# All matmuls of the middle units as 64x64 tiles, and the last projection piece in token halves

## The chip, the core and the metric

The kernel runs on one core of a Trainium2 chip. The metric is the device time of one launch in microseconds (us), as the median of several runs; lower is better. The core has a matrix engine (TensorE, PE in the profile, whose weight loads have a row of their own, PEld), a vector engine (VectorE, DVE), a scalar engine (ScalarE, ACT), a general engine (GpSimd, POOL) and a queue engine (SyncE, SP) that here only starts transfers. Each takes its instructions in the order in which the program gives them and waits at each for semaphores. TensorE writes to PSUM, from where only VectorE and ScalarE read; everything else lies in SBUF or in device memory.

## The reference

The input is 8 sequences of 4,096 tokens of 192 values. A causal convolution over 7 tokens runs along each sequence, with softmax weights that the 24 channels of a head share; then every token goes through a gated feed-forward layer:

```python
out = np.einsum('hk,bskhg->bshg', softmax(weight), windows_of_7(x))   # 8 heads, 7 taps
x = out.reshape(32768, 192)
gate = np.maximum(x @ w_gate, 0.0)        # 192 -> 1536
val = x @ w_val                           # 192 -> 1536
result = (gate * val) @ w_out             # 1536 -> 192
```

The kernel computes in fp16 with fp32 sums.

## The kernel before, in words

The sequences are taken in pairs, one of the lower four and one of the upper four, called streams: their channels lie one above the other in the 128 partitions, 64 of the one and 64 of the other, in three chunks of 64 channels. The work is cut into 16 units of 1,024 tokens of both streams, numbered 0 to 15, each of two windows of 512 tokens. Units 0 and 15 take paths of their own (`project`); units 1 to 14 are the middle units and all alike.

A unit's gate and value products (`gate_val`, once per window) go over 12 blocks of 128 hidden features. For each block there are two PSUM tiles of two banks, one for the gate and one for the value, a bank for each stream. For each chunk and stream one matmul (L547) multiplies 64 channels by 128 features over 512 tokens. The two streams' matmuls lie in the upper and the lower 64 rows of the array and run side by side; I call what runs side by side a step. A step is 2 matmuls, a block 6 steps. Then ScalarE takes the gate's tile through a relu to fp16 (gr, L558), and VectorE multiplies it with the value's tile (hT, L559).

The projection of a middle unit (`project_across`, L723) multiplies by w_out with features as the contraction, and gives the output with channels in partitions. Its three pieces are two PSUM banks each: a is channels 0 to 127 of window 0, b is the same of window 1 (both `wide_pass`, L644, 64x128 tiles), c is channels 128 to 191 of both windows (`narrow_pass`, L664, 64x64 tiles, four side by side). A piece has 128 features in each of 12 blocks, 64 in the upper and 64 in the lower rows of the array. As two row halves may not write to one bank at once, a piece is made in two turns: in the first the upper rows write to bank 0 and the lower to bank 1, in the second the other way round. A no-operation on SyncE (L686) stands between the turns of a piece. The order of the passes is written out at L727: a's first turn, c's first, a's second, b's first, c's second, b's second. After its second turn a piece is copied from PSUM to SBUF as 16-bit words in two planes (`words`, L690): a and c by ScalarE alone, b by ScalarE for bank 0 and VectorE for bank 1. SyncE then writes them to the device buffer held, and during the next unit brings them back transposed and sends them out.

Beside this, ScalarE, VectorE and GpSimd make the convolution of the units that come next. ScalarE starts sums (L507) and multiplies by taps (products, L491): ten products stand in its queue ahead of the copy of a and six ahead of the copy of c. VectorE goes on with the sums (L521) and makes five products (L493), the last two of them behind its copy of b (L759). GpSimd adds the products up (L497).

PSUM has four tiles of two banks, handed out in turn. At the end of a unit the next unit's first block takes the tile that is free and a's; its second block takes c's and, for its value, b's. The third block's value takes the tile that the first block's value had, and so waits for the first hT.

Of the kernel before, what the change touches and what calls it, by code (L numbers as in the profile page):

```python
# [9 lines left out]
F16 = mybir.dt.float16  # L10
I32 = mybir.dt.int32
U16 = mybir.dt.uint16
# [5 lines left out]
def kernel(  # L18
# [12 lines left out]
    nc = tc.nc  # L31

    B, S, D = x.shape
# [5 lines left out]
    NCH = D // 64  # L39
    NBLK = D // 32  # L40
    NFF = DFF // 128
    WIN = 512
# [9 lines left out]
    NUNIT = NB * S // UNIT  # L52
# [11 lines left out]
    xpool = ctx.enter_context(tc.tile_pool(name="xpool", bufs=2))  # L64
# [3 lines left out]
    ypool = ctx.enter_context(tc.tile_pool(name="ypool", bufs=1))  # L68
# [7 lines left out]
    ROOM = 4 * WIN  # L76
# [25 lines left out]
    SYNC = mybir.DependencyInfo(mybir.DependencyClass.Sync, mybir.DependencyReason.DATA)  # L102
# [20 lines left out]
    def body(st):  # L123
# [11 lines left out]
        out=xts[0][PAD : PAD + FIRST, 0, :, :],  # L135
# [27 lines left out]
    Wo = const.tile([128, NFF, D], F16)  # L163
# [94 lines left out]
    same = const.tile([SUB, SEG], F16)  # L258
# [228 lines left out]
    def product(engine, v, c, k):  # L487
        out = prods[v][:, k, c, :]
        in_, scale = shifted(v, c, k, 1), tap[:, c, k : k + 1]
        if engine is nc.scalar:  # L490
            engine.activation(out=out, in_=in_, func=ACTF.Copy, scale=scale)  # L491
        else:
            engine.tensor_scalar(out=out, in0=in_, scalar1=scale, scalar2=None, op0=ALU.mult)  # L493
# [40 lines left out]
    def gate_val(u, w):  # L534
        h = hpool.tile([128, NFF, 2, WIN], F16, name="hT")
        xcb = xc[u]
        for f in range(NFF):
            if u == 0 and w == 0 and f == 5:
                second_block()
            pss = [psum.tile([128, 2, 512], FP, name="ps") for _ in range(2)]  # L540
            order = [(i, c) for i in range(2) for c in range(NCH)]
            if u == 0 and w == 0 and f == 0:
                order = [(i, c) for c in range(NCH) for i in range(2)]
            for i, c in order:
                W = (Wg, Wv)[i]
                for st in range(2):
                    nc.tensor.matmul(  # L547
                        out=pss[i][:, st, :],
                        lhsT=W[64 * st : 64 * st + 64, c, 128 * f : 128 * (f + 1)],
                        rhs=xcb[64 * st : 64 * st + 64, c, WIN * w : WIN * (w + 1)],  # L550
                        start=(c == 0),
                        stop=(c == NCH - 1),
                        tile_position=(64 * st, 0),
                    )
            by_stream = u == 0 and w == 0 and f < 2
            for sts in (slice(0, 1), slice(1, 2)) if by_stream else (slice(0, 2),):
                gr = gpool.tile([128, 2, WIN], F16, name="gr")
                nc.scalar.activation(out=gr[:, sts], in_=pss[0][:, sts], func=ACTF.Relu)  # L558
                nc.vector.tensor_tensor(  # L559
                    out=h[:, f, sts], in0=gr[:, sts], in1=pss[1][:, sts], op=ALU.mult  # L560
                )
        return h
# [78 lines left out]

    across, planes = {}, {}

    def wide_pass(hs, w, ps, turn, after):  # L644


        for f in range(NFF):
            for r in range(2):
                st = r ^ turn
                mm = nc.tensor.matmul(  # L650
                    out=ps[:, st, :],
                    lhsT=Wo[64 * r : 64 * r + 64, f, 0:128],
                    rhs=hs[w][64 * r : 64 * r + 64, f, st, :],
                    start=(turn == 0 and f == 0),
                    stop=(turn == 1 and f == NFF - 1),
                    tile_position=(64 * r, 0),
                    skip_group_check=True,
                )
                if after is not None:
                    tc.add_manual_dep(mm.ins, after.ins.name, SYNC, reason="same banks, other rows")  # L660
                    after = None
        return turn_over(turn, mm)

    def narrow_pass(hs, ps, turn, after):  # L664
        for f in range(NFF):
            for r in range(2):
                w = r ^ turn
                for st in range(2):
                    mm = nc.tensor.matmul(  # L669
                        out=ps[64 * st : 64 * st + 64, w, :],  # L670
                        lhsT=Wo[64 * r : 64 * r + 64, f, 128:D],
                        rhs=hs[w][64 * r : 64 * r + 64, f, st, :],
                        start=(turn == 0 and f == 0),
                        stop=(turn == 1 and f == NFF - 1),
                        tile_position=(64 * r, 64 * st),
                        skip_group_check=True,
                    )
                    if after is not None:
                        tc.add_manual_dep(mm.ins, after.ins.name, SYNC, reason="same banks, other rows")
                        after = None  # L680
        return turn_over(turn, mm)

    def turn_over(turn, mm):
        if turn:
            return None
        done = nc.sync.nop()  # L686
        tc.add_manual_dep(done.ins, mm.ins.name, SYNC, reason="first turn over")
        return done

    def words(ps, ways):  # L690
        pool, name = (ypool, "y") if len(ways) > 1 else (xpool, "x_h")
        flat = pool.tile([128, ROOM], F16, name=name)
        pt = flat[:].bitcast(U16).rearrange("p (b l t) -> p b l t", b=2, l=2)
        from_ = ps[:].bitcast(U16).rearrange("p b (t l) -> p b l t", l=2)
        step = 2 // len(ways)
        for j, copy in enumerate(ways):
            part = slice(step * j, step * j + step)
            copy(out=pt[:, part], in_=from_[:, part])  # L698
        return pt.rearrange("p b l t -> p b (l t)")

    def turn_back(u, i):
        w, st = i // 2, i % 2
        os_ = opool.tile([128, 4, D], FP, name="out_s")
        nc.sync.dma_start_transpose(
            out=os_[:].bitcast(U16),
            in_=planes[u][w, st].rearrange("c (l t) -> (c l) t", l=2),
        )
        across[u, i] = os_

    def send(u, i):  # L710
        w, st = i // 2, i % 2
        bp, w0 = u * UNIT // S, u * UNIT % S // WIN
        row0 = (bp + NB * st) * S + WIN * (w0 + w)
        nc.sync.dma_start(
            out=bass.AP(
                tensor=out.tensor,
                offset=out.offset + row0 * D,
                ap=[[D, 128], [128 * D, 4], [1, D]],
            ),
            in_=across.pop((u, i))[:],  # L720
        )

    def project_across(u, hs, work):  # L723
        held = planes[u] = dram.tile([2, 2, D, 2 * WIN], U16, name="held")
        at, done = {}, {}
        back = u - 1 in planes
        for i, turn in [("a", 0), ("c", 0), ("a", 1), ("b", 0), ("c", 1), ("b", 1)]:  # L727
            if turn == 0:
                at[i] = psum.tile([128, 2, 512], FP, name="ps")
            else:  # L730
                for c, k in work["acb".index(i)]:
                    product(nc.scalar, u + 1, c, k)
            if i == "c":
                done[i] = narrow_pass(hs, at[i], turn, done.get(i))
            else:
                done[i] = wide_pass(hs, int(i == "b"), at[i], turn, done.get(i))
            if back and turn == 0:
                if i == "a":
                    turn_back(u - 1, 3)
                elif i == "c":  # L740
                    send(u - 1, 2)
                else:
                    send(u - 1, 3)
            if turn == 0:
                continue
            if i == "c":
                pt = words(at[i], (nc.scalar.copy,))
                for st in range(2):
                    nc.sync.dma_start(
                        out=held[:, st, 128:D, :].rearrange("w c e -> c w e"),  # L750
                        in_=pt[64 * st : 64 * st + 64],
                    )
                continue
            ways = (nc.scalar.copy,) if i == "a" else (nc.scalar.copy, nc.vector.tensor_copy)
            pt = words(at[i], ways)
            nc.sync.dma_start(
                out=held[int(i == "b"), :, 0:128, :].rearrange("s c e -> c s e"), in_=pt
            )
        if u + 2 < NUNIT:  # L759
            for c, k in VECTOR[3:]:  # L760
                product(nc.vector, u + 1, c, k)
# [151 lines left out]
```

## Time and profile before

| | us |
|---|---|
| median of 3 runs | 784.92 |
| lowest, highest | 784.05, 791.28 |
| the profiled execution | 783.54 |
| its span | 781.7 |
| TensorE busy | 766.5 |
| VectorE busy | 711.9 |
| ScalarE busy | 624.6 |
| GpSimd busy | 378.8 |

The span runs from the first to the last instruction of the profiled execution, whose own time holds 1.84 us more. Matmuls are pipelined and their ends are modelled, so two that run side by side or one after another overlap in the rows, and a busy share of TensorE says little about how fast it streams. For that one divides the time of a long row in the chain by the number of its steps. The chain follows the work that ended last back from the end, each time to what released it.

### The profile page before, as it was taken

Reading aid. Unit: us, or ns where it says so; the run is one execution under the profiler, and the core shown is the slowest. Engines: PE = TensorE matmul, PEld = TensorE weight load, DVE = VectorE, ACT = ScalarE, POOL = GpSimd, SP = SyncE. Lnnn points to the kernel's source line nnn. Section 1 sums busy time; section 2 is a strip of 40 time slices with the busy share of each in tenths; the row PEclk is TensorE's granted clock in tenths of the full one; section 3 lists DMA queues with packets and bytes.
Section 4 is the critical chain, followed back from the end, with each engine's and each line's share of the span. In section 5 each row is a group of like instructions: output and inputs, shape, how many; then the busy total and the mean of one; then the engine's idle time right before and its main releaser. Section 6 shows DMA issues by size and latency. Waiting matters only on the chain.

```text
span 781.7 us, 19814 instructions
## 1 busy us (share of the span) xinstructions
PE 766.5 (98%) x8247; PEld 403.7 (52%) x8247; DVE 711.9 (91%) x768; ACT 624.6 (80%) x719; POOL 378.8 (48%) x249
## 2 busy tenths in 40 slices
PE   9999999999999999999999999999999999999998
PEld 5495445454454544545445454454544545455458
DVE  7999999999999998999989999899998999999891
ACT  6787877979788797887978879788797887975672
POOL 9529358092571916619165290753908438081000
PEclk9999999999999999999999999999999999999999
DMA  9969049486594955849668495694948738353732
GB/s 115 129 123 130 1 103 170 132 113 134 128 164 142 111 150 116 151 143 131 150 107 143 141 145 136 115 147 126 159 123 126 148 122 155 109 131 84 181 83 82
DMA packets 231266, 99.65 MB, mean 127 GB/s; under 512 B 185288, under 2 KB 220424, under 8 KB 231176
## 3 DMA queue, kind: packets, MB, share of 16 engines
q1 hardware_dynamic: 189928, 82.71, 48.1%
q0 software_dynamic: 41104, 15.57, 20.1%
q8 instruction: 64, 1.05, 0.6%
q14 instruction: 26, 0.21, 0.1%
q10 hardware_dynamic: 144, 0.10, 0.0%
HBM read 31.48 MB, written 47.19 MB: 101 GB/s over the span
## 4 chain that ended last, share of the span: by engine, by line
PE 92%; DVE 4%; ACT 2%; issue 2%; DMA 1%; POOL 0%; POOLq 0%
PE ps L547 58%; PE ps L650 19%; PE ps L669 10%; PE ps L576 3%; DVE hT L559 2%; ACT y L698 2%; DVE prods L493 1%; PE ps L625 1%; DVE y L698 1%; DMA x_h<-in_x_dram 1%; PE ps L369 0%; PE ps L410 0%; ACT acc L602 0%; POOL steps L132 0%; POOLq L132 0%
## 5 line engine op out<-in xcount | busy, mean ns | idle before, releaser
L559 DVE TENSOR_TENSOR hT<-gr,ps 128x1024 f16<-128x1024 f16 (+1 forms) x386 | 466.3, 1214 | 31.0 <-ACT gr L558 6.9
L558 ACT ACTIVATE gr<-ps 128x1024 f16<-128x1024 f32 (+1 forms) x386 | 393.0, 1019 | 112.4 <-PE ps L547 112.0
L497 POOL TENSOR_TENSOR prods<-prods 128x1344 f32<-128x1344 f32 x70 | 212.2, 3031 | 308.1 <-DVE prods L493 234.9
L547 PE MATMUL ps<-xc,Wv 64*128 64x512 f16 x2304 | 317.3, 376 | 10.8 <-DVE y L698 5.9
L547 PE MATMUL ps<-xc,Wg 64*128 64x512 f16 x2304 | 317.1, 376 | 0.0
L547 PEld LDWEIGHTS <-Wv 64*128 64x128 f16 x2304 | 136.5, 94 | 127.8 <-issue 19.0
L547 PEld LDWEIGHTS <-Wg 64*128 64x128 f16 x2304 | 127.7, 94 | 120.6 <-issue 0.3
L521 DVE SCALAR_TENSOR_TENSOR acc<-x_r,tap,acc 128x576 f32<-128x576 f16 x225 | 165.3, 809 | 0.0
L650 PE MATMUL ps<-hT,Wo 64*128 64x512 f16 x1344 | 152.4, 376 | 0.0
L491 ACT ACTIVATE prods<-x_r,tap 128x448 f32<-128x448 f16 x222 | 127.3, 659 | 0.0
L650 PEld LDWEIGHTS <-Wo 64*128 64x128 f16 x1344 | 65.8, 94 | 81.9 <-issue 11.5
L669 PE MATMUL ps<-hT,Wo 64*64 64x512 f16 x1344 | 78.0, 378 | 0.0
L698 ACT COPY x_h<-ps 128x2048 uint16<-128x2048 uint16 x28 | 52.2, 1865 | 10.8 <-PE ps L650 5.6
L669 PEld LDWEIGHTS <-Wo 64*64 64x64 f16 x1344 | 36.8, 107 | 39.6 <-issue 11.9
L207 POOL DMA_DIRECT2D x_e<-in_x_dram x58 | 47.0, 821 | 15.4 <-ACT acc L507 11.6
L471 POOL COPY x_p<-x_e 128x960 f16<-128x960 f16 (+1 forms) x58 | 50.3, 906 | 0.9 <-DMA x_e<-in_x_dram 0.8
L497 POOL TENSOR_TENSOR xc<-prods 128x1344 f16<-128x1344 f32 x14 | 42.4, 3030 | 1.1
L521 DVE SCALAR_TENSOR_TENSOR xc<-x_r,tap,acc 128x576 f16<-128x576 f16 x45 | 34.0, 808 | 0.0
L698 DVE COPY y<-ps 128x1024 uint16<-128x1024 uint16 x14 | 17.1, 1224 | 18.0 <-ACT y L698 18.0
L507 ACT ACTIVATE acc<-x_r,tap 128x576 f32<-128x576 f16 x45 | 31.4, 763 | 0.0
L493 DVE TENSOR_SCALAR prods<-x_r,tap 128x448 f32<-128x448 f16 x70 | 27.5, 443 | 0.0
L576 PE MATMUL ps<-Wo,hT 64*128 64x192 f16 x576 | 24.6, 243 | 0.0
(63 smaller groups left out, 119.1 us busy)
## 6 DMA issues: line engine op xcount, KB each, us to landing
out_dram<-out_s SPq DMA_DIRECT2D x62, 384.0 KB, 3.2
held<-x_h SPq DMA_DIRECT2D x14, 512.0 KB, 3.1
held<-x_h SPq DMA_DIRECT2D x28, 256.0 KB, 3.2
held<-y SPq DMA_DIRECT2D x14, 512.0 KB, 3.1
x_e<-in_x_dram POOLq DMA_DIRECT2D x34, 192.0 KB, 7.2
x_e<-in_x_dram POOLq DMA_DIRECT2D x24, 240.0 KB, 5.5
x_r<-x_p SPq DMA_TRANSPOSE x131, 4.6
out_s<-held SPq DMA_TRANSPOSE x56, 4.7
```

The source lines that it names most:

```text
L207: first = nc.gpsimd.dma_start(out=xe[:, j0 + start : j0 + n, st, :, :].rearrange("p j c r -> p j (c r)"), in_=bass.AP(tensor=x.tensor, off ...
L471: nc.gpsimd.tensor_copy(out=xp[:, j0 : j0 + n, :, st, :], in_=xe[:, j0 : j0 + n, st, :, :])
L491: engine.activation(out=out, in_=in_, func=ACTF.Copy, scale=scale)
L497: nc.gpsimd.tensor_tensor(out=pr[:, 0] if k < KW - 1 else xc[v + 1][:, :, LDVE:UNIT], in0=pr[:, 0], in1=pr[:, k], op=ALU.add,)
L521: nc.vector.scalar_tensor_tensor(out=xc[v][:, c, 0:LDVE] if k == KW - 1 else acc[:, c, :], in0=shifted(v, c, k, 0), scalar=tap[:, c, k : k ...
L547: nc.tensor.matmul(out=pss[i][:, st, :], lhsT=W[64 * st : 64 * st + 64, c, 128 * f : 128 * (f + 1)], rhs=xcb[64 * st : 64 * st + 64, c, WI ...
L558: nc.scalar.activation(out=gr[:, sts], in_=pss[0][:, sts], func=ACTF.Relu)
L559: nc.vector.tensor_tensor(out=h[:, f, sts], in0=gr[:, sts], in1=pss[1][:, sts], op=ALU.mult)
L576: mm = nc.tensor.matmul(out=outs[q], lhsT=h[64 * r : 64 * r + 64, f, st, 128 * q : 128 * (q + 1)], rhs=Wo[64 * r : 64 * r + 64, f, :], sta ...
L650: mm = nc.tensor.matmul(out=ps[:, st, :], lhsT=Wo[64 * r : 64 * r + 64, f, 0:128], rhs=hs[w][64 * r : 64 * r + 64, f, st, :], start=(turn ...
L669: mm = nc.tensor.matmul(out=ps[64 * st : 64 * st + 64, w, :], lhsT=Wo[64 * r : 64 * r + 64, f, 128:D], rhs=hs[w][64 * r : 64 * r + 64, f, ...
L698: copy(out=pt[:, part], in_=from_[:, part])
```

## The change

In units 1 to 14 every matmul is of 64x64 tiles. In `gate_val` each matmul of 64 channels by 128 features becomes two of 64 features, in the left and the right half of the array, so that a step is four matmuls. The two passes of the projection become one, `cross_pass`, that takes the piece as a number (0 is a, 1 is b, 2 is c) and a range of tokens; a and b are now made of halves of 64 channels as well. The order of the passes is the same.

The second turn of b is made in two halves of 256 tokens, each with its own 48 matmuls. The first half of the tokens is read out of both banks by ScalarE after the first half's matmuls. After the second half's, ScalarE reads the rest of bank 0 and VectorE the rest of bank 1. The first readout and the second half's matmuls touch the same two banks. The copies of a and c, the products and the transfers keep their places.

```diff
@@ gate_val
+            M = 64 if 0 < u < NUNIT - 1 else 128
             for i, c in order:
                 W = (Wg, Wv)[i]
                 for st in range(2):
-                    nc.tensor.matmul(
-                        out=pss[i][:, st, :],
-                        lhsT=W[64 * st : 64 * st + 64, c, 128 * f : 128 * (f + 1)],
+                    for m in range(0, 128, M):
+                        nc.tensor.matmul(
+                            out=pss[i][m : m + M, st, :],
+                            lhsT=W[64 * st : 64 * st + 64, c, 128 * f + m : 128 * f + m + M],
...
-                        tile_position=(64 * st, 0),
+                            tile_position=(64 * st, m),
@@ wide_pass and narrow_pass become
+    def cross_pass(piece, hs, ps, turn, after, cols=slice(0, WIN)):
         for f in range(NFF):
             for r in range(2):
+                bank = r ^ turn
+                for half in range(2):
+                    if piece == 2:
+                        w, st, d = bank, half, 128
+                    else:
+                        w, st, d = piece, bank, 64 * half
                     mm = nc.tensor.matmul(
+                        out=ps[64 * half : 64 * half + 64, bank, cols],
+                        lhsT=Wo[64 * r : 64 * r + 64, f, d : d + 64],
+                        rhs=hs[w][64 * r : 64 * r + 64, f, st, cols],
...
+                        tile_position=(64 * r, 64 * half),
...
+    def words(copy, pt, ps, banks, t0, t1):
+        copy(
+            out=pt[:, banks, :, t0:t1],
+            in_=ps[:, banks, t0:t1].bitcast(U16).rearrange("p b (t l) -> p b l t", l=2),
+        )
@@ project_across, second turns
+            if i == 1:
+                cross_pass(1, hs, at[1], 1, done[1], slice(0, half))
+                words(nc.scalar.copy, pt, at[1], both, 0, half)
+                cross_pass(1, hs, at[1], 1, None, slice(half, WIN))
+                words(nc.scalar.copy, pt, at[1], slice(0, 1), half, WIN)
+                words(nc.vector.tensor_copy, pt, at[1], slice(1, 2), half, WIN)
+            else:
+                cross_pass(i, hs, at[i], 1, done[i])
+                words(nc.scalar.copy, pt, at[i], both, 0, WIN)
```

More of the change, by code (lines that the diff above doesn't have):

```diff
@@ L546, in gate_val @@
                 for st in range(2):
-                    nc.tensor.matmul(
-                        out=pss[i][:, st, :],
-                        lhsT=W[64 * st : 64 * st + 64, c, 128 * f : 128 * (f + 1)],
-                        rhs=xcb[64 * st : 64 * st + 64, c, WIN * w : WIN * (w + 1)],
-                        start=(c == 0),
-                        stop=(c == NCH - 1),
-                        tile_position=(64 * st, 0),
-                    )
+                    for m in range(0, 128, M):
+                        nc.tensor.matmul(
+                            out=pss[i][m : m + M, st, :],
+                            lhsT=W[64 * st : 64 * st + 64, c, 128 * f + m : 128 * f + m + M],
+                            rhs=xcb[64 * st : 64 * st + 64, c, WIN * w : WIN * (w + 1)],
+                            start=(c == 0),
+                            stop=(c == NCH - 1),
+                            tile_position=(64 * st, m),
+                        )
             by_stream = u == 0 and w == 0 and f < 2
@@ L642 @@
     across, planes = {}, {}
-    def wide_pass(hs, w, ps, turn, after):
+    def cross_pass(piece, hs, ps, turn, after, cols=slice(0, WIN)):
         for f in range(NFF):
             for r in range(2):
[L649 to L668, printed above, removed]
+                bank = r ^ turn
[4 more added lines that the diff above has]
+                        w, st, d = piece, bank, 64 * half
                     mm = nc.tensor.matmul(
-                        out=ps[64 * st : 64 * st + 64, w, :],
-                        lhsT=Wo[64 * r : 64 * r + 64, f, 128:D],
-                        rhs=hs[w][64 * r : 64 * r + 64, f, st, :],
+                        out=ps[64 * half : 64 * half + 64, bank, cols],
+                        lhsT=Wo[64 * r : 64 * r + 64, f, d : d + 64],
+                        rhs=hs[w][64 * r : 64 * r + 64, f, st, cols],
                         start=(turn == 0 and f == 0),
                         stop=(turn == 1 and f == NFF - 1),
-                        tile_position=(64 * r, 64 * st),
+                        tile_position=(64 * r, 64 * half),
                         skip_group_check=True,
@@ L688, in turn_over @@
         return done
[L690 to L699, printed above, removed]
+    def words(copy, pt, ps, banks, t0, t1):
+        copy(
+            out=pt[:, banks, :, t0:t1],
+            in_=ps[:, banks, t0:t1].bitcast(U16).rearrange("p b (t l) -> p b l t", l=2),
+        )
     def turn_back(u, i):
@@ L726, in project_across @@
         back = u - 1 in planes
-        for i, turn in [("a", 0), ("c", 0), ("a", 1), ("b", 0), ("c", 1), ("b", 1)]:
+        both, half = slice(0, 2), WIN // 2
+        for i, turn in [(0, 0), (2, 0), (0, 1), (1, 0), (2, 1), (1, 1)]:
             if turn == 0:
                 at[i] = psum.tile([128, 2, 512], FP, name="ps")
-            else:
[L731 to L747, printed above, removed]
+                done[i] = cross_pass(i, hs, at[i], 0, None)
+                if back:
+                    if i == 0:
+                        turn_back(u - 1, 3)
+                    elif i == 2:
+                        send(u - 1, 2)
+                    else:
+                        send(u - 1, 3)
+                continue
+            for c, k in work[(0, 2, 1)[i]]:
+                product(nc.scalar, u + 1, c, k)
+            pool, name = (ypool, "y") if i == 1 else (xpool, "x_h")
+            pt = pool.tile([128, 2, 2, WIN], U16, name=name)
+            if i == 1:
[4 more added lines that the diff above has]
+                words(nc.vector.tensor_copy, pt, at[1], slice(1, 2), half, WIN)
+            else:
+                cross_pass(i, hs, at[i], 1, done[i])
+                words(nc.scalar.copy, pt, at[i], both, 0, WIN)
+            flat = pt[:].rearrange("p b l t -> p b (l t)")
+            if i == 2:
                 for st in range(2):
@@ L750, in project_across @@
                         out=held[:, st, 128:D, :].rearrange("w c e -> c w e"),
-                        in_=pt[64 * st : 64 * st + 64],
+                        in_=flat[64 * st : 64 * st + 64],
                     )
[L753 to L758, printed above, removed]
+            else:
+                nc.sync.dma_start(out=held[i, :, 0:128, :].rearrange("s c e -> c s e"), in_=flat)
         if u + 2 < NUNIT:
```

## The prediction

> **What bounds the kernel now.** I read the totals first, then the chain that ended last, then one boundary between two units, engine by engine.
>
> ```profile
> PE 766.5 (98%) x8247; PEld 403.7 (52%) x8247; DVE 711.9 (91%) x768; ACT 624.6 (80%) x719; POOL 378.8 (48%) x249
> ...
> PE 92%; DVE 4%; ACT 2%; issue 2%; DMA 1%; POOL 0%; POOLq 0%
> ```
>
> TensorE is busy for 98% of the span and holds 92% of the chain; the other 8% are short pieces. The chain shows where they lie. Its columns are start, length (both us), and the line with its instruction count; this is one of the fourteen middle units.
>
> ```profile
> 301.18 28.02 PE ps L547 x258
> 329.20 2.59 PE ps L650 x24
> 331.79 2.71 PE ps L669 x48
> 334.50 5.29 PE ps L650 x48
> 339.79 2.71 PE ps L669 x48
> 342.50 2.71 PE ps L650 x24
> ...
> 349.41 28.02 PE ps L547 x258
> ```
>
> A unit lasts 349.41 - 301.18 = 48.23 us. Between its gate matmuls (L547) and those of the next lie the six projection passes, which I call a0, c0, a1, b0, c1 and b1 in their order (a1 and b0 share the row of 5.29). Two things in it are not arithmetic. A wide pass that follows work of its own shape takes 2.59 us (a0); each pass that follows the other shape takes 0.12 more: 2.71 for c0, c1 and b1, and 5.29 = 2 x 2.59 + 0.11 for a1 with b0. So four changes of tile shape cost 0.47 us a unit. The second thing is the boundary:
>
> ```profile
> 345.03 0.81 PE L547 MATMUL ps<-xc,Wg 64*128 64x512 f16 x6
> 345.68 0.81 PE L547 MATMUL ps<-xc,Wv 64*128 64x512 f16 x6
> 346.33 0.81 PE L547 MATMUL ps<-xc,Wg 64*128 64x512 f16 x6
> 347.56 0.82 PE L547 MATMUL ps<-xc,Wv 64*128 64x512 f16 x6 [0.42 <-DVE y L698]
> 348.20 0.83 PE L547 MATMUL ps<-xc,Wg 64*128 64x512 f16 x6
> 349.41 0.39 PE L547 MATMUL ps<-xc,Wv 64*128 64x512 f16 x2 [0.38 <-DVE hT L559]
> ```
>
> Groups of six start 0.65 us apart, but the fourth comes 1.23 after the third and the sixth 1.21 after the fifth: two stalls of 0.58 and 0.56 (the bracketed idle is smaller because modelled ends overlap). The fourth group waits for b's PSUM tile, which VectorE reads last; the sixth waits for the first hT, which VectorE makes only after that copy.
>
> ```profile
> 346.28 1.22 DVE L698 COPY y<-ps 128x1024 uint16<-128x1024 uint16 x1 [1.21 <-ACT y L698]
> 347.43 0.81 DVE L493 TENSOR_SCALAR prods<-x_r,tap 128x448 f32<-128x448 f16 x2
> 348.15 1.21 DVE L559 TENSOR_TENSOR hT<-gr,ps 128x1024 f16<-128x1024 f16 x1
> ```
>
> VectorE's copy waits for ScalarE's copy of the other bank, so the two run one after the other.
>
> **The change: no gain in arithmetic.** Four 64x64 tiles fill the same array as two 64x128 tiles, so a step still streams 512 columns. The narrow passes already run so, and their steady pace can be read from two moments two steps apart, with the weight loads of one step:
>
> ```profile
> 56.95 31.08 PE ps L547 x288
> 762.74 7.92 PE ps L576 x192
> 331.96 0.60 PE L669 MATMUL ps<-hT,Wo 64*64 64x512 f16 x8
> 331.96 0.12 PEld L669 LDWEIGHTS <-Wo 64*64 64x64 f16 x4
> 332.39 0.60 PE L669 MATMUL ps<-hT,Wo 64*64 64x512 f16 x8
> ...
> 14.21 1.52 PE ps L369 x120
> ```
>
> Pairs of 512 columns take 31.08 / 144 = 0.216 us; quads take (332.39 - 331.96) / 2 = 0.215. I cost the 2,016 gate steps and 840 full projection steps of the fourteen units at nothing; half a nanosecond of rounding each way would be 1.4 us. All units' passes now have one shape, so the 0.47 us go.
>
> The half passes of b1 have 256 columns, which no row shows. Pairs of 192 columns take 7.92 / 96 = 0.0825, pairs of 512 take 0.216: on the line through both, 256 columns take 0.109. Bounds: 0.107 (slope alone) and 0.12 (the burst of four weight loads above, if nothing of it hid). I take 0.109: the last row is a convolution whose 120 matmuls, each with a weight load of its own, pass in 1.52 us, 79 loads a us, and a half step asks for 37. A half pass of 12 quads then takes 1.31 us.
>
> **The new wait.** In the changed program's instruction order, the first matmul of the second half stands like this:
>
> ```
> 3630 L657 Matmult ps<-hT,Wo 64x256
> 3631 L657 Ldweights Wo
> 3632 L657 Matmult ps<-hT,Wo 64x256 [waits Activation_49]
> ```
>
> It waits for ScalarE's count after the readout of the first half, which lies in the same two banks. So this readout does not run beside the second half: TensorE stands still for it, and queued behind it are the second half and all gate matmuls of the next unit. VectorE's third part still waits for ScalarE alone, as its row above does. Behind the readouts wait, on ScalarE, the next unit's first gr; on VectorE two products (then GpSimd's adds, which are not on the chain) and the first hT; on SyncE the write of b to held.
>
> When does ScalarE begin that readout? Its own rows:
>
> ```profile
> 329.51 2.09 ACT L507 ACTIVATE acc<-x_r,tap 128x576 f32<-128x576 f16 x3
> 331.51 5.70 ACT L491 ACTIVATE prods<-x_r,tap 128x448 f32<-128x448 f16 x10
> 337.24 1.86 ACT L698 COPY x_h<-ps 128x2048 uint16<-128x2048 uint16 x1
> 339.00 3.46 ACT L491 ACTIVATE prods<-x_r,tap 128x448 f32<-128x448 f16 x6
> 342.55 1.86 ACT L698 COPY x_h<-ps 128x2048 uint16<-128x2048 uint16 x1
> 345.24 1.01 ACT L698 COPY y<-ps 128x1024 uint16<-128x1024 uint16 x1 [0.82 <-PE ps L650]
> ```
>
> From 329.51 on it is full. Neighbours without a wait overlap by about 0.1 (337.24 + 1.86 = 339.10, next start 339.00). The copy of a waited 0.12 for TensorE (337.12 would do), c's waited 0.18 (342.37). With three changes of shape gone before c1 ends, TensorE gives c at 342.50 - 0.35 = 342.15, and ScalarE can take it at 342.37 - 0.12 = 342.25. It cannot be earlier. So ScalarE gains 0.30 us, not 0.47:
>
> - c's copy: 342.25 to 344.11. First half pass: done at 342.15 + 1.31 = 343.46, hence not what is waited for.
> - First readout, 1,024 elements as in today's y row (1.01): 344.01 to 345.02.
> - TensorE resumes 0.06 later (347.56 against VectorE's end at 346.28 + 1.22 today): 345.08. The second half ends its issue at 346.39, where the next unit's gate matmuls start. Today: 345.03. **The boundary starts 1.36 us late.**
>
> Then the prices of the shorter copies:
>
> ```profile
> L698 ACT COPY x_h<-ps x28: 1865/1865/1866, 96.1 to 728.4; 128x2048 uint16<-128x2048 uint16 x28
> L698 ACT COPY y<-ps x14: 1012/1012/1012, 104.1 to 731.1; 128x1024 uint16<-128x1024 uint16 x14
> L698 DVE COPY y<-ps x14: 1223/1224/1225, 105.1 to 732.1; 128x1024 uint16<-128x1024 uint16 x14
> L559 DVE TENSOR_TENSOR hT<-gr,ps x386: 678/1221/1223, 9.5 to 763.2; 128x1024 f16<-128x1024 f16 x191, 128x512 f16<-128x512 f16 x2
> ```
>
> On ScalarE 1,024 elements more cost 853 ns, so 512 take 1012 - 427 = 585 ns (bounds 506, half of today's, and 1012). On VectorE an instruction with half the elements takes 678 instead of 1221; I take 680 for 512 (bounds 612 and 1224).
>
> - Second half's results: today ScalarE starts 0.21 after TensorE turned to the gate matmuls (345.24 - 345.03), so 346.60. ScalarE to 347.19; VectorE 347.21 to 347.89.
> - The fourth gate group wants to start at 346.39 + 3 x 0.65 = 348.34: its stall is gone.
> - The first hT starts 0.65 after the copy's end, as today (347.50 to 348.15): 348.54, and ends at 349.75. The sixth group wants to start at 346.39 + 5 x 0.65 = 349.63 and gets 349.79; today 349.41.
>
> So the new wait takes 1.36, the shorter readout gives back most of the two stalls (1.14 today, 0.16 left), and the unit is 0.38 us longer. The 0.47 us of the shape changes are inside this sum: they move b1 forward to where it waits for ScalarE. Fourteen boundaries: 5.3 us; I cost the last, into unit 15, like the others. Two changes of shape remain, into unit 1 and into unit 15: 0.24. Rounded with 0.03 a unit for matmuls that restart one by one behind the wait: 783.54 (the profiled execution, span 781.7) + 6 = 789.5. The median of the runs shown, 784.92, lies 1.4 higher; on it the sum gives **791**.
>
> A rule of the Trainium skill speaks against the half passes: by "TensorE: Matmul & The Clock Gate", section "LDWEIGHTS (loading the stationary operand)", a load takes its columns divided by 1.2 in ns. Four loads of 64 columns, one after another, would by that estimate take 213 ns, as long as a 512-column step and twice a half step. The trace does not bear it out as a sum: four loads lie within 0.12 us in the row at 331.96.
>
> **The rivals.**
> 1. *Weight loads bind the half steps.* If four loads had to follow each other, quads would take about 0.21 whatever their width: four rows of 0.107 us would have to share the array in pairs. The first half would be done at 344.71, the readout at 345.76, the second half at 348.4, and the sixth gate group at about 351.8: 2.4 us a unit, 34 in all, 819 on the median. Against it: the burst of 0.12.
> 2. *The quads run slower over long stretches.* Instructions per us double for all of a unit and not for 2.7 us. One to 3 ns a step over 2,856 steps are 3 to 9 us more: 794 to 800. No row shows more than 48 quad matmuls in a row.
> 3. *The shape is not what the 0.12 us are for* (the change does not do what it says). Then c1 and b1 stay where they are, ScalarE gains nothing, and a unit is 0.30 longer: 795. Against it: a1 to b0 changes the piece and not the shape, and their row has room for one 0.11 only.
> 4. *Faster: TensorE is not held at the middle of b1.* Place: the first readout. If ScalarE ended it before the first half pass leaves TensorE at about 343.3, the second half would start at once, the gate matmuls at 344.6, and both stalls would go: 1.4 us a unit gained, 765. The deciding point is ScalarE's end at 345.02 in my sum: every 0.1 us earlier gives 1.4 us, and break-even is 344.6. Against it: its rows are full from 329.51 on.
>
> **How the numbers follow.** Forecast 0.62 (787 to 797 with the copies' and ScalarE's bounds), rival 1 0.05, rival 2 0.15, rival 3 0.08, rival 4 0.06; 0.04 for the unseen. The range 786 to 801 leaves out rivals 1 and 4 and some tails. A measurement of this kernel tells about 1% (8 us) from no change. Slower by more: rivals 1 and 3, most of 2, and a fifth of the forecast's own range, 0.38. Faster: rival 4, 0.06. The rest, 0.56, within 1%.
>
> **What would show it.** In the changed profile: no pass longer than 2.6 us except b1; a TensorE idle of some 1.5 us in each b1 that ends with ScalarE's first y copy; y copies of about 1.01, 0.59 and 0.68 us; the wait of gate matmuls for VectorE's y gone and the one for hT smaller; a unit of about 48.6 us. I am wrong if the unit is under 48.2 (then ScalarE came earlier), if half steps take over 0.12, or if gate groups of 12 stand further apart than 0.65 us.

## The result, and the profile after

The change makes the kernel slower: a median of 790.55 us (789.7 to 794.38, 20 runs) against 784.56 (783.62 to 791.31, 20 runs). The ratio is 1.0071, with a 95% interval of 1.0054 to 1.0088; it compares the means of all the runs, and the medians alone give 1.0076. The profiled execution took 789.98 us, with a span of 788.2. Two of the 20 runs of the kernel before lie at 791.3 us, 0.9% above its median, so single runs of the two kernels overlap and only the many runs tell them apart.

The page of the changed kernel, totals and chain:

```profile
PE 761.1 (97%) x14295; PEld 504.5 (64%) x14295; DVE 706.0 (90%) x768; ACT 630.3 (80%) x733; POOL 379.9 (48%) x249
...
PE 67%; ACT 26%; issue 2%; DMA 2%; SPq 2%; POOL 0%; ACTq 0%; DVE 0%; POOLq 0%
```

TensorE's part of the chain fell from 92% to 67%, and ScalarE's rose from 2% to 26%. ScalarE works hardly more than before (630.3 us against 624.6); it has come to lie on the path. Where, the timeline of one boundary shows, ScalarE first:

```profile
331.88 2.10 ACT L507 ACTIVATE acc<-x_r,tap 128x576 f32<-128x576 f16 x3
333.88 5.69 ACT L491 ACTIVATE prods<-x_r,tap 128x448 f32<-128x448 f16 x10
339.48 1.85 ACT L679 COPY x_h<-ps 128x2048 uint16<-128x2048 uint16 x1
341.22 3.47 ACT L491 ACTIVATE prods<-x_r,tap 128x448 f32<-128x448 f16 x6
344.59 1.85 ACT L679 COPY x_h<-ps 128x2048 uint16<-128x2048 uint16 x1
346.34 1.01 ACT L679 COPY y<-ps 128x1024 uint16<-128x1024 uint16 x1
348.95 0.59 ACT L679 COPY y<-ps 128x512 uint16<-128x512 uint16 x1 [1.60 <-PE ps L657]
```

TensorE at the same boundary, from the second half of b's second turn to the sixth gate group:

```profile
347.40 1.50 PE L657 MATMUL ps<-hT,Wo 64*64 64x256 f16 x48 [1.58 <-ACT y L679]
348.71 0.84 PE L549 MATMUL ps<-xc,Wg 64*64 64x512 f16 x12
349.36 0.84 PE L549 MATMUL ps<-xc,Wv 64*64 64x512 f16 x12
350.00 0.84 PE L549 MATMUL ps<-xc,Wg 64*64 64x512 f16 x12
350.65 0.84 PE L549 MATMUL ps<-xc,Wv 64*64 64x512 f16 x12
351.30 0.84 PE L549 MATMUL ps<-xc,Wg 64*64 64x512 f16 x12
352.17 0.84 PE L549 MATMUL ps<-xc,Wv 64*64 64x512 f16 x12
```

And VectorE:

```profile
349.57 0.69 DVE L679 COPY y<-ps 128x512 uint16<-128x512 uint16 x1 [2.11 <-ACT y L679]
350.18 0.81 DVE L493 TENSOR_SCALAR prods<-x_r,tap 128x448 f32<-128x448 f16 x2
350.90 3.57 DVE L561 TENSOR_TENSOR hT<-gr,ps 128x1024 f16<-128x1024 f16 x3
```

ScalarE runs without a break from 331.88 to the end of its first y copy at 347.35; 0.05 later TensorE goes on, after 1.58 us of standing still. This is the new wait. The copies behind it are short, and of the two old stalls only 0.22 is left, ahead of the sixth group (351.30 to 352.17 is 0.87, where its own pace is 0.65).

The chain puts ScalarE's products on the path as well, but they are not what makes the wait. At the last such boundary, into unit 15, ScalarE has no products to make and stands idle before each of its copies of a and c; the wait is as long:

```profile
728.50 1.87 ACT L679 COPY x_h<-ps 128x2048 uint16<-128x2048 uint16 x1 [5.40 <-PE ps L657]
733.68 1.87 ACT L679 COPY x_h<-ps 128x2048 uint16<-128x2048 uint16 x1 [3.31 <-PE ps L657]
735.45 1.02 ACT L679 COPY y<-ps 128x1024 uint16<-128x1024 uint16 x1
736.51 1.50 PE L657 MATMUL ps<-hT,Wo 64*64 64x256 f16 x48 [1.57 <-ACT y L679]
```

The copy of c takes 1.87 us and TensorE's half pass 1.31, so the half is done while ScalarE still copies c, and the readout of 1.02 us comes after that.

### The profile page after: what moved, and what is told of

Same layout as the page of the kernel before. It is cut to its first block, busy times and chain, and to the rows that moved or that the text cites. A ratio compares the mean times of both kernels' runs of the same rounds, so it can differ in the third digit from the quotient of the medians.

```text
span 788.2 us, 31924 instructions
## 1 busy us (share of the span) xinstructions
PE 761.1 (97%) x14295; PEld 504.5 (64%) x14295; DVE 706.0 (90%) x768; ACT 630.3 (80%) x733; POOL 379.9 (48%) x249
## 4 chain that ended last, share of the span: by engine, by line
PE 67%; ACT 26%; issue 2%; DMA 2%; SPq 2%; POOL 0%; ACTq 0%; DVE 0%; POOLq 0%
PE ps L549 59%; ACT prods L491 15%; ACT x_h L679 6%; PE ps L657 4%; ACT acc L507 3%; PE ps L578 3%; ACT y L679 2%; SPq L475 1%; DMA out_s<-held 1%; PE ps L627 1%; DMA x_h<-in_x_dram 0%; PE ps L369 0%; POOL x_p L471 0%; ACTq L491 0%; POOL x_h L133 0%
## 5 line engine op out<-in xcount | busy, mean ns | idle before, releaser
L549 PE MATMUL ps<-xc,Wv 64*64 64x512 f16 (+1 forms) x4320 | 322.8, 376 | 0.3
L549 PE MATMUL ps<-xc,Wg 64*64 64x512 f16 (+1 forms) x4320 | 322.8, 376 | 0.0
L657 PE MATMUL ps<-hT,Wo 64*64 64x512 f16 (+1 forms) x4704 | 223.4, 346 | 22.1 <-ACT y L679 22.1
L549 PEld LDWEIGHTS <-Wv 64*64 64x64 f16 (+1 forms) x4320 | 154.3, 105 | 97.3 <-issue 4.6
L549 PEld LDWEIGHTS <-Wg 64*64 64x64 f16 (+1 forms) x4320 | 157.0, 106 | 89.2 <-issue 0.4
L657 PEld LDWEIGHTS <-Wo 64*64 64x64 f16 x4704 | 157.1, 107 | 88.6 <-issue 24.8
L679 ACT COPY y<-ps 128x1024 uint16<-128x1024 uint16 (+1 forms) x28 | 22.4, 801 | 22.4 <-PE ps L657 22.4
L679 DVE COPY y<-ps 128x512 uint16<-128x512 uint16 x14 | 9.7, 692 | 30.6 <-ACT y L679 30.6
L578 PEld LDWEIGHTS <-hT 64*128 64x128 f16 x576 | 23.9, 94 | 0.5
```

The source lines that it names most:

```text
L549: nc.tensor.matmul(out=pss[i][m : m + M, st, :], lhsT=W[64 * st : 64 * st + 64, c, 128 * f + m : 128 * f + m + M], rhs=xcb[64 * st : 64 * ...
L578: mm = nc.tensor.matmul(out=outs[q], lhsT=h[64 * r : 64 * r + 64, f, st, 128 * q : 128 * (q + 1)], rhs=Wo[64 * r : 64 * r + 64, f, :], sta ...
L657: mm = nc.tensor.matmul(out=ps[64 * half : 64 * half + 64, bank, cols], lhsT=Wo[64 * r : 64 * r + 64, f, d : d + 64], rhs=hs[w][64 * r : 6 ...
L679: copy(out=pt[:, banks, :, t0:t1], in_=ps[:, banks, t0:t1].bitcast(U16).rearrange("p b (t l) -> p b l t", l=2),)
```

## The experiments

The theory: b's second half is held until ScalarE has read the first, and ScalarE comes to that late because it still has c to copy; the shapes by themselves are worth 0.12 us for each change of shape, and a quad costs what a pair costs. The rivals: the price lies in the quads or in their weight loads, or the 0.12 us are for something else. The kernel before, run again beside these kernels, has a median of 784.28 us (19 runs) beside the first four and 783.95 us (17 runs) beside the last two. Lengths of a unit below are taken between two sixth gate groups in each kernel's chain; the kernel before has 48.23 us and the full change 352.17 - 303.53 = 48.64 by its own chain:

```profile
303.53 27.41 PE ps L549 x504
...
352.17 27.41 PE ps L549 x504
```

**b undivided.** The full change, with b's second turn in one pass again:

```diff
-                cross_pass(1, hs, at[1], 1, done[1], slice(0, half))
-                words(nc.scalar.copy, pt, at[1], both, 0, half)
-                cross_pass(1, hs, at[1], 1, None, slice(half, WIN))
-                words(nc.scalar.copy, pt, at[1], slice(0, 1), half, WIN)
-                words(nc.vector.tensor_copy, pt, at[1], slice(1, 2), half, WIN)
+                cross_pass(1, hs, at[1], 1, done[1])
+                words(nc.scalar.copy, pt, at[1], slice(0, 1), 0, WIN)
+                words(nc.vector.tensor_copy, pt, at[1], slice(1, 2), 0, WIN)
```

> All matmuls of the middle units stay 64x64 tiles, but b's second turn is undivided again and read out as before (ScalarE bank 0, then VectorE bank 1). Theory (the wait inside b costs the time, the shape changes are worth 0.47 us a unit): no TensorE idle inside b, all six passes 2.59 us, b's results 0.47 us earlier and everything behind them too; unit 47.76 us, 784.6 - 14 x 0.47 + 0.24 = 778.2. Rival (the 0.12 us a pass are not for the shape): the time of the kernel before, 784.6. Rival (quads run slower over long stretches, by 1 to 3 ns a step): 781 to 787.

Measured: 778.1 us, ratio to the kernel before 0.993 (0.9911 to 0.9949). Its chain:

```profile
327.14 15.56 PE ps L657 x288
342.70 0.02 issue
342.73 1.02 ACT y L679
...
346.90 28.04 PE ps L549 x516
...
394.70 5.34 PE ps L549 x93
```

All six passes stand in one row of 15.56 us, 0.45 under the 2.59 + 2.71 + 5.29 + 2.71 + 2.71 = 16.01 of the kernel before, with no wait in it. A unit is 394.70 - 346.90 = 47.80 us. So the 64x64 shapes save what the changes of shape cost, and the cut of b alone turned that gain into a loss: 790.55 against 778.1.

**The cut alone.** The shapes of the kernel before, with only b's second turn cut:

```diff
...
+        wide_pass(hs, 1, ps, 1, after, slice(0, half))
+        part(nc.scalar.copy, both, 0, half)
+        wide_pass(hs, 1, ps, 1, None, slice(half, WIN))
+        part(nc.scalar.copy, slice(0, 1), half, WIN)
+        part(nc.vector.tensor_copy, slice(1, 2), half, WIN)
...
```

> The shapes of the kernel before everywhere, but b's second turn in two token halves, read out in three parts. Theory: c's copy still starts at 342.55 on the clock of the unit shown, the first readout ends at 345.32, the second half leaves TensorE at 346.69, the sixth gate group starts 0.69 us later than before: 784.6 + 9.7 = 794.2, slower than the full change because ScalarE does not gain its 0.30 us. Rival (the 64x64 tiles or their many weight loads are what costs, the wait is harmless): 779 to 785.

Measured: 794.36 us, ratio 1.0128 (1.0114 to 1.0143). TensorE at the boundary, by the timeline:

```profile
346.26 1.48 PE L650 MATMUL ps<-hT,Wo 64*128 64x256 f16 x24
349.21 1.49 PE L650 MATMUL ps<-hT,Wo 64*128 64x256 f16 x24 [1.47 <-ACT y L706]
```

The wait is there with pairs in b as with quads. The rival that the quads bring the loss falls: with pairs in the gate, a and b it is larger by 3.8 us, 0.27 a unit, where 0.30 was worked out for what ScalarE does not gain.

**A later cut.** The same change, cut at 384 tokens:

```diff
-        both, half = slice(0, 2), WIN // 2
+        both, half = slice(0, 2), 3 * WIN // 4
```

> The full change with b's second turn cut at 384 tokens in place of 256. Theory: first part of 384 columns done at 344.10, first readout 1.44 us long, to 345.58; the second part's quads of 128 columns cost 0.056 us, so 0.67 in all; the last two copies 0.37 and 0.42 us; the gate's own pace then decides, the sixth group starts 0.17 us later than before: 787.3, some 3 us under the full change. Rival (weight loads bind narrow quads at 0.12 us each): the second part takes 1.44 us, 797 to 798.

Measured: 786.6 us, ratio 1.0031 (1.002 to 1.0042). TensorE by the timeline, and ScalarE:

```profile
346.32 0.86 PE L657 MATMUL ps<-hT,Wo 64*64 64x128 f16 x48 [1.54 <-ACT y L679]
346.99 0.85 PE L549 MATMUL ps<-xc,Wg 64*64 64x512 f16 x12
```

```profile
344.83 1.44 ACT L679 COPY y<-ps 128x1536 uint16<-128x1536 uint16 x1
347.23 0.37 ACT L679 COPY y<-ps 128x256 uint16<-128x256 uint16 x1 [0.96 <-PE ps L657]
```

Twelve quads of 128 columns pass in 346.99 - 346.32 = 0.67 us, 0.056 each, with four weight loads in each. Weight loads do not bind here, even at a quarter of the columns. The wait is as long as in the full change (1.54 against 1.58), and less work stands behind it. The time is 0.7 us under what was expected.

**c's copy on two engines.** The full change, with c's later tokens copied by VectorE:

```diff
-                words(nc.scalar.copy, pt, at[i], both, 0, WIN)
+                words(nc.scalar.copy, pt, at[i], both, 0, half if i == 2 else WIN)
+                if i == 2:
+                    words(nc.vector.tensor_copy, pt, at[i], both, half, WIN)
```

> The full change, but c's copy is shared: ScalarE copies the first 256 tokens of both banks, VectorE the other 256 in the time in which it waits for b. Theory (what TensorE waits for inside b is ScalarE being late with c's copy): the first readout can start when b's first half is done, 0.51 us earlier; the idle inside b falls from 1.58 to about 1.07 us, the unit by 0.49: 783.7. Rival (the wait is for something else than ScalarE's queue, or the end is set elsewhere): 790.6.

Measured: 783.69 us, ratio to the kernel before 0.9981 (0.9961 to 1.0002). ScalarE and TensorE by the timeline:

```profile
342.14 0.99 ACT L679 COPY x_h<-ps 128x1024 uint16<-128x1024 uint16 x1
343.43 1.01 ACT L679 COPY y<-ps 128x1024 uint16<-128x1024 uint16 x1 [0.29 <-PE ps L657]
```

```profile
344.49 1.50 PE L657 MATMUL ps<-hT,Wo 64*64 64x256 f16 x48 [1.11 <-ACT y L679]
```

Now ScalarE waits for TensorE's first half (0.29), and TensorE's own wait is 1.11 in place of 1.58: the 0.47 that went was ScalarE's lateness with c. What is left of the wait is the readout itself and its way there and back, and it can't go while the second half has to follow the first readout. No run here lets the two go on side by side, so whether anything but the program's order asks for it stays open.

**b undivided, products first.** The undivided b pointed at VectorE's queue, which waits there for ScalarE and has two products to make after its copy. They were moved ahead of it:

```diff
                 words(nc.scalar.copy, pt, at[1], slice(0, 1), 0, WIN)
+                if u + 2 < NUNIT:
+                    for c, k in VECTOR[3:]:
+                        product(nc.vector, u + 1, c, k)
                 words(nc.vector.tensor_copy, pt, at[1], slice(1, 2), 0, WIN)
...
-        if u + 2 < NUNIT:
-            for c, k in VECTOR[3:]:
-                product(nc.vector, u + 1, c, k)
```

> As whole_b, with VectorE's last two products moved ahead of its copy of b, into the time in which it waits for ScalarE. Theory (at the boundary VectorE's queue, copy then products then hT, sets when the sixth gate group starts): VectorE's copy starts as before, hT follows it at once 0.7 us earlier, the sixth group needs no wait; the stall of the fourth stays. 0.56 us a unit in 13 units: 778.1 - 7.3 = 770.8. Rival (the products delay the copy, so the fourth group's stall grows by what the sixth's loses): 778.

Measured: 770.44 us, ratio 0.9809 (0.9774 to 0.9844), the fastest of all and better than both kernels. ScalarE's copy of b, VectorE and TensorE by the timeline:

```profile
340.14 1.01 ACT L679 COPY y<-ps 128x1024 uint16<-128x1024 uint16 x1 [0.71 <-PE ps L657]
339.27 1.90 DVE L493 TENSOR_SCALAR prods<-x_r,tap 128x448 f32<-128x448 f16 x5
341.19 1.23 DVE L679 COPY y<-ps 128x1024 uint16<-128x1024 uint16 x1
342.33 1.21 DVE L561 TENSOR_TENSOR hT<-gr,ps 128x1024 f16<-128x1024 f16 x1
```

```profile
341.19 0.84 PE L549 MATMUL ps<-xc,Wg 64*64 64x512 f16 x12
342.46 0.84 PE L549 MATMUL ps<-xc,Wv 64*64 64x512 f16 x12 [0.43 <-DVE y L679]
343.11 0.84 PE L549 MATMUL ps<-xc,Wg 64*64 64x512 f16 x12
343.76 0.84 PE L549 MATMUL ps<-xc,Wv 64*64 64x512 f16 x12
```

The products end as ScalarE's copy does (341.17 and 341.15), VectorE's copy follows, and the sixth group comes 0.65 after the fifth: its stall is gone. The fourth's is left. The cut of b went for the same two stalls by making the readout shorter, and put a longer one in their place.

**Gate alone.** Only `gate_val` in 64x64 tiles, everything else as before:

```diff
+            M = 64 if 0 < u < NUNIT - 1 else 128
...
+                    for m in range(0, 128, M):
...
+                            out=pss[i][m : m + M, st, :],
+                            lhsT=W[64 * st : 64 * st + 64, c, 128 * f + m : 128 * f + m + M],
...
+                            tile_position=(64 * st, m),
```

> Only the gate and value matmuls of the middle units as 64x64 tiles; the projection and its readout as in the kernel before. Theory (a quad step costs what a pair step costs; a change of shape costs 0.12 us): six changes a unit in place of four; the one into a0 is on the path, the one from b1 into the gate disappears in the stall behind it. 784.6 + 14 x 0.12 = 786.2. Rival (the 0.12 us are not for the shape): 784.6. Rival (64x64 tiles are quicker by themselves, and whole_b's gain came from them): 780 or less.

Measured: 786.75 us, ratio 1.0025 (1.0000 to 1.0051). By the ratio alone this can't be told from no change; its chain tells it:

```profile
303.04 28.04 PE ps L549 x516
331.07 2.70 PE ps L652 x24
333.77 2.71 PE ps L671 x48
...
351.40 28.04 PE ps L549 x516
```

The pass of a0 now follows another shape and takes 2.70 in place of 2.59. The gate's 129 steps take 28.04 us, against 28.02 for the 129 steps of pairs. The unit is 48.36 us, 0.13 longer. Fourteen times 0.13 is 1.8 us, and the profiled execution is 3.0 us longer than that of the kernel before. Another 1.1 of it lies ahead of unit 1, whose gate starts in the chain at 58.08 in place of 56.95; no run here says why.

## Why the prediction was right

The forecast of 791, slower by 0.8%, came out at 790.55, and each step can be laid beside its row. Both boundaries are put on one clock by the first of ScalarE's sums (329.51 before, 331.88 after, so 2.37 is taken off):

| step | forecast | measured |
|---|---|---|
| c's copy begins | 342.25 | 342.22 |
| first readout of b begins | 344.01 | 343.97 |
| TensorE resumes | 345.08 | 345.03 |
| next unit's gate begins | 346.39 | 346.34 |
| ScalarE's second readout | 346.60, 0.585 long | 346.58, 0.59 long |
| VectorE's part | 347.21, 0.68 long | 347.20, 0.69 long |
| first hT | 348.54 | 348.53 |
| sixth gate group | 349.79 | 349.80 |

- *No gain in arithmetic.* The gate's rows after (27.41 us for 126 steps in the chain, 0.2175 with the tail of the last) and those of the kernel with the gate alone (28.04 us for 129 steps, against 28.02) show quads at the pace of pairs: 0.2 ns a step are lost, where rival 2 (slower over long stretches) needed 1 to 3. It falls.
- *0.47 us a unit for changes of shape.* Shown by the undivided b (0.43 a unit, 6 us in all) and, for one change, by the gate alone. Rival 3 falls.
- *Half steps at 0.109.* 348.71 - 347.40 = 1.31 us for twelve. That quarter steps cost 0.056 disposes of rival 1. The Trainium skill has a rule for the loss of speed in the load: by "TensorEngine Tiling (Array Packing)", section "Restrictions and Gotchas", column tiling can't go with the fast weight load. The rows agree that a load is slower (107 ns for 64 columns, 94 for 128 before); it lies beside the matmuls and costs nothing here.
- *The new wait, 1.36 us a unit at the start of the gate.* The gate begins at 346.34, against 345.03 in the kernel before: 1.31. The cut alone, with pairs in b and the gate, has the same wait. That part of it is ScalarE being late with c is shown by c's copy on two engines: 0.47 less wait, 783.69 where 783.7 was expected. Rival 4 cannot happen as it was put: the readout reads the first half's results, so it cannot end before that half leaves TensorE. What was held against it, that ScalarE's rows are full, does not decide it either, as the boundary into unit 15 shows with the same wait behind idle time. Its break-even of 344.6 for the readout's end fits: with c's copy on two engines the end lies at 343.43 + 1.01 = 344.44, which is 344.51 on the clock of the table (its first sum starts at 329.44), and a unit is 48.17 us (301.08 to 349.25 in its chain) against 48.23 before.
- *The stalls that go.* 1.14 to 0.22, where 0.16 was forecast. VectorE's row waits for ScalarE as in the kernel before, and both queues are priced as they stand.

That the late start came out 0.05 smaller and the stall that is left 0.06 larger is one and the same thing: the sixth group goes by the first hT, which came when it was forecast. The unit is 48.64 us, 0.41 longer, as 0.38 and the 0.03 for a slow restart give it. The 0.03 is right by luck: no row shows that restart (the twelve half steps behind the wait take 1.31 us, their full pace), and 0.02 of it is the gate's own 28.04 against 28.02.

One term was too small. The boundary into unit 15 was costed like the others, at 0.38 with 0.12 for the change of shape. From the sixth gate group of unit 14 to the end of unit 15's gate it is 76.55 us in the chain (692.65 to 769.20) against 75.70 before (687.04 to 762.74): 0.85. VectorE has no products there, so the kernel before had only the stall of the fourth group to lose (its sixth follows its fifth by 0.65, 734.07 to 734.72). With 0.2 us at the kernel's start, which no term had, the profiled execution is 6.4 us longer where the sum said 6; the medians are 6.0 apart. The 1% that the prediction asked for to tell a change from none was too much: with 20 runs each, 0.7% is told.

## What to carry to other kernels

A readout in parts brings something only if the engine that reads is free when the part is ready, and if the work that goes on does not have to wait for it (no run here had the second); two passes into the same banks with a readout between them are a wait of a whole copy, there and back. Before a copy is cut, the order of the queue that holds the waiting work should be looked at: two products moved ahead of a copy that waited anyway gave 7.7 us, and the cut took 12.5. A gain of one engine counts only up to the next wait: of the 0.47 us of shapes 0.35 came ahead of c's copy, and ScalarE's queue let 0.30 of them through.

## What the runs showed of the hardware

Nothing went against what had been worked out from the rows. New as a measurement is the pace of narrow quads: with 64x64 tiles, a weight load in front of every matmul, a step of 256 columns takes 0.109 us and one of 128 columns 0.056, so that the line through the pairs of 192 and 512 columns holds down to 128, although each load's own row lasts 0.107 us. A change between 64x128 and 64x64 tiles costs 0.11 to 0.12 us (a0 takes 2.70 behind the other shape and 2.59 behind its own), and the undivided b, without the changes between passes, has all six in 15.56 us in place of 16.01.
